# The end of an attention and MoE kernel: one sum in another buffer, the last stores in other queues

## The chip, the cores and the metric

The kernel runs on one core of a Trainium2 chip. The metric is the device time of one execution in microseconds, as a median of several. Before the change it is 204.68 us (three runs, 204.35 to 205.12). The core has a matrix engine (TensorE, PE in the profile; PEld are its weight loads), VectorE (DVE), ScalarE (ACT), GpSimd (POOL) and SyncE (SP), which here only issues DMAs. Each engine works through its own stream of instructions in order, and streams wait for each other by semaphores. DMAs are issued from a stream and then run beside it.

## The reference

There are 8 batches with 8 heads of 512 tokens and 32 state rows, 64 wide. Tokens attend to state rows and state rows to tokens; the results of both go through a two-layer network with a GELU.

```python
scores = scale * np.matmul(x, state.transpose(0, 1, 3, 2))
a = softmax(scores)                    # written out in the reference
xread = np.matmul(a, state)            # 512 rows for each batch and head
sread = np.matmul(softmax(scale * np.matmul(state, x.transpose(0, 1, 3, 2))), x)   # 32 rows
rows = concatenate([xread, sread])     # 8 * 544 = 4352 rows of 512
out = gelu(rows @ w_in) @ w_out        # 512 -> 2048 -> 512
```

The output is 4352 x 512 in float32, 8.9 MB.

## The kernel before

A unit of work is one batch b. For it the kernel builds the attention weights (AT) and a product P of the state with w_in, so that `mm1` gets the hidden rows directly from AT and P; ScalarE's GELU writes them to the tile `g` (128 partitions, 16 blocks of the hidden size, 512 tokens). The second layer multiplies `g` by w_out. From the second unit on this is done by quarters with seven products instead of eight: `X(b, name)` with names "1" to "7" is one product of half the tokens with half the hidden size by half of the output columns (16 matmuls with 256 columns). Some of the products need a sum or difference of two quarters of `g` as their left side. `g_sum(b, names)` makes it on VectorE (1.2 us each) in a tile `gsum` from a pool of three buffers (`apool`); within a unit the order is "5", "6", "7", "3". Sum "3" is made from a quarter of `g` and sum "6". In the last unit sum "3" gets the same buffer as sum "7", which product "7" reads, so the sum waits until product "7" has been read through.

The products gather in PSUM banks. ScalarE copies intermediate states out (`snap`: c2, c4, u, s5), and VectorE adds bank and copy into the output tiles `oh`: `xs[b, "o", 0]` and `xs[b, "o", 1]`, each with two row blocks j and 512 columns. An output quarter is one half tile's left or right 256 columns: 256 KB. `c21` makes the left quarter of half 1 from product "7" and c4, `c22` the right quarter of half 1 from product bank 1 and s5. `x_out` stores quarters over SyncE's queue.

`R(name)` does the same seven products for the 256 rows of state reads, in tiles `osb`, stored by `r_out` over SyncE.

The change is in the last unit, b = 7. Its end is written out by hand (lines 1215 to 1227): sums "5" and "6", product "1", sum "7", R("7"), product "6", sum "3", R("3"), product "7", c21 and its store, then `L5` and `L3`. These two do the products "5" and "3" in three pieces each (`PIECES`): row block 0 with 256 columns, then row block 1 in two halves of 128 columns, so that copies, additions and stores can begin early. In `L5`, ScalarE copies each piece; as soon as a row block is complete, c22 adds it, and 128 KB go out. In `L3`, VectorE adds each piece with u, and the piece goes out: 128, 64 and 64 KB.

The streams of the engines keep the order in which the lines stand, up to small shifts between queues. A DMA on SyncE's or ScalarE's queue is tied to one of eight semaphores in turn, and before it is issued its queue waits until the DMA eight places before has landed. When all work is issued, SyncE waits for every semaphore in a fixed row, and a barrier of all engines ends the program; these records stand at line 1253.

Of the kernel before, what the change touches and what calls it, by code (L numbers as in the profile page):

```python
# [10 lines left out]
BF16 = mybir.dt.bfloat16  # L11
# [6 lines left out]
def kernel(  # L18
# [8 lines left out]
    nc = tc.nc  # L27
# [17 lines left out]
    apool = ctx.enter_context(tc.tile_pool(name="apool", bufs=3))  # L45
# [36 lines left out]
    x4s = [persist.tile([128, SJ, HC, 128], BF16, name=f"x4_{i}") for i in range(2)]  # L82
# [474 lines left out]
    MH = MC // 2  # L557
    NH = d_model // 2
# [23 lines left out]
    left, right = slice(0, NH), slice(NH, d_model)  # L582
# [8 lines left out]
    def g_q(b, h, k):  # L591
        return gs[b][:, MH * k:MH * k + MH, 256 * h:256 * h + 256]

    def chain(name, q, got):
        a11, a12, a21, a22 = q(0, 1), q(0, 0), q(1, 1), q(1, 0)
        return {
            "1": (a11,),
            "2": (a12,),
            "4": (a22,),
            "5": (a21, a22, ALU.add),  # L600
            "6": (got.get("5"), a11, ALU.subtract),
            "7": (a11, a21, ALU.subtract),
            "3": (a12, got.get("6"), ALU.subtract),
        }[name]

    g_lhs = {}

    def g_sum(b, names):
        got = g_lhs.setdefault(b, {})
        for name in names:  # L610
            x, y, op = chain(name, lambda h, k: g_q(b, h, k), got)
            got[name] = apool.tile([128, MH, 256], BF16, name="gsum", tag="gsum")
            nc.vector.tensor_tensor(out=got[name], in0=x, in1=y, op=op)  # L613

    def x_lhs(b, name):
# [16 lines left out]
    def c_tile(name):  # L632
        return cpool.tile([128, 2, NH], FP32, name=name, tag=name)
# [7 lines left out]
    def add(out, x, y):  # L641
        nc.vector.tensor_tensor(out=out, in0=x, in1=y, op=ALU.add)  # L642
# [5 lines left out]
    def X(b, name):  # L648
        bank = BANK[name]
        first = name in "2154"  # L650
        if first:
            xs[b, bank] = otile([128, 2, NH], "xp", bank)
        ps = xs[b, bank]
        x_mm(ps, x_lhs(b, name), w_rhs(name), first)
        if name == "2":
            if b > 1:
                snap(b, "c2", "c2", ps)
        elif name == "4":
            snap(b, "c4", "c4", ps)
        elif name == "1":  # L660
            for h in range(2):
                xs[b, "o", h] = hpool.tile([128, 2, d_model], FP32, name="oh", tag=f"oh{h}")
            add(xs[b, "o", 0][:, :, left], ps, xs[b, "c2"])
            x_out(b, 0, left)
        elif name == "6":
            snap(b, "u", "u", ps)
        elif name == "5":
            snap(b, "s5", "s5", ps)
        elif name == "7":
            if b < B - 2:  # L670
                c22(b)
                c21(b)
                x_out(b, 1)
        elif name == "3":
            add(xs[b, "o", 0][:, :, right], ps, xs[b, "u"])
            x_out(b, 0, right)

    def c22(b, js=slice(0, 2)):
        add(xs[b, "o", 1][:, js, right], xs[b, 1][:, js, :], xs[b, "s5"][:, js, :])
# [4 lines left out]
    def rows_out(h, js, ns, eng):  # L684
        b = B - 1
        rows = out[b * SB:b * SB + S, :].rearrange("(p j) n -> p j n", j=SJ)
        eng.dma_start(
            out=rows[:, 2 * h + js.start:2 * h + js.stop, ns], in_=xs[b, "o", h][:, js, ns]
        )
# [3 lines left out]
    def l_mm(name, first):  # L693
        b = B - 1
        lhs, rhs = x_lhs(b, name), w_rhs(name)
        for j, n0, n1, at in PIECES:
            if first:
                xs[b, "x", j, n0] = otile([128, n1 - n0], "xp", at)
            ps = xs[b, "x", j, n0]
            for m in range(MH):  # L700
                nc.tensor.matmul(  # L701
                    ps,
                    lhsT=lhs[:, m, 128 * j:128 * j + 128],
                    rhs=rhs[:, m, n0:n1],
                    start=(first and m == 0),
                    stop=(m == MH - 1),
                    skip_group_check=True,
                )
            yield ps, j, n0, n1

    def L5():
        b = B - 1
        xs[b, "s5"] = c_tile("s5")
        for ps, j, n0, n1 in l_mm("5", True):
            nc.scalar.copy(out=xs[b, "s5"][:, j, n0:n1], in_=ps)
            if n1 == NH:
                c22(b, slice(j, j + 1))
                rows_out(1, slice(j, j + 1), right, nc.sync)

    def L3():  # L720
        b = B - 1
        for ps, j, n0, n1 in l_mm("3", False):
            add(xs[b, "o", 0][:, j, NH + n0:NH + n1], ps, xs[b, "u"][:, j, n0:n1])
            rows_out(
                0, slice(j, j + 1), slice(NH + n0, NH + n1), nc.scalar if n0 else nc.sync
            )

    sr = {}
# [114 lines left out]
    def R(name):  # L843
        def c_new(n):
            rs[n] = cpool.tile([128, NH], FP32, name="r_" + n, tag="r_" + n)
            return rs[n]

        bank = BANK[name]
        first = name in "2154"
        if first:  # L850
            home = {"2": 1, "4": 2}
            rs[bank] = otile([128, NH], "rp", home[name]) if name in home else ftile([128, NH], "rp")
        ps = rs[bank]
        lhs = chain(name, r_q, {})[0] if name in "124" else rs["lhs"][name]
        rhs = w_rhs(name)
        for m in range(MH):
            nc.tensor.matmul(  # L857
                ps,
                lhsT=lhs[:, m, :],
                rhs=rhs[:, m, :],  # L860
                start=(first and m == 0),
                stop=(m == MH - 1),
                skip_group_check=True,
            )
        snaps = {"2": "c2", "4": "c4", "6": "u", "5": "s5"}
        if name in snaps:
            nc.scalar.copy(out=c_new(snaps[name]), in_=ps)
        elif name == "1":
            for h in range(2):
                rs["o", h] = opool.tile([128, d_model], FP32, name="osb", tag="osb")  # L870
            add(rs["o", 0][:, left], ps, rs["c2"])
        elif name == "7":
            add(rs["o", 1][:, right], ps, rs["s5"])
            add(rs["o", 1][:, left], ps, rs["c4"])
            r_out(1)
        elif name == "3":
            add(rs["o", 0][:, right], ps, rs["u"])
            r_out(0)
# [69 lines left out]
    def read_out_slot(p):  # L948
        c, b, k = B - 2, B - 1, 16 * (B - 1) + 2 * p
        if p == 0:  # L950
            sr_x("34")
            M(k, k + 1)
            g_sum(c, "56")
            SR("3", 0)
            SR("4", 0)
            X(c, "1")
            sr_x("167")
            SR("5", 0)
            SR("2", 0)
            sr_w("7")  # L960
# [6 lines left out]
        if p == 2:  # L967
            M(k, k + 1)
            SR_gelu("6", 0)
            SR("7", 0)  # L970
            SR_gelu("7", 0)
            g_sum(c, "7")
            X(c, "5")
            SR("3", 1)
            SR("4", 1)
            g_sum(c, "3")
# [238 lines left out]
    b = B - 1  # L1215
# [2 lines left out]
    g_sum(b, "7")  # L1218
    R("7")
    X(b, "6")  # L1220
    g_sum(b, "3")
    R("3")
    X(b, "7")
    c21(b)
    x_out(b, 1, left)
    L5()
    L3()


# [28 lines left out]
```

## Time and profile before

| | us |
|---|---|
| median of three runs | 204.68 |
| the profiled execution, whole | 204.74 |
| its span in the profile | 202.84 |
| TensorE busy | 194.0 |
| last matmul ends | 197.99 |
| last addition ends | 198.30 |
| last store issued (SyncE) | 199.13 |
| last landing | 201.48 |

The difference between the whole and the span, 1.9 us, lies outside of what the profile records. All times in the text count from the span's start. A line of a group names the source line, the engine, the operation, the tiles (out<-in), the shape and the count; a trailing [2.82 <-PE xp L623] says that the engine was idle 2.82 us before it and what ended that. SPq and ACTq are the DMA-issuing records of SyncE and ScalarE; the time to landing is from issue until the semaphore has its last count. TensorE's granted clock was 0.998 of full speed.

### The profile page before, as it was taken

To read this page: it belongs to the slowest core of one execution; us is meant where nothing else is said; L and a number is where in the kernel's file an instruction comes from. 1 tells how busy PE (TensorE), PEld (TensorE's weight loads), DVE (VectorE), ACT (ScalarE), POOL (GpSimd) and SP (SyncE) were. 2 spreads that over 40 slices of the span, in tenths; PEclk is the share of its full clock that TensorE was granted. 3 is DMA by queue.
4 is the path that set the end of the run, shared out by engine and by line. 5 is a ranking of instruction groups with operands and counts; after the bars stand their busy time and mean duration, and the time that the engine had idled before them with its cause. 6 is when DMAs were issued, how large, how long until landed. Compare 5 with 4: busy or idle time off the path is not lost.

```text
span 202.8 us, 4863 instructions
## 1 busy us (share of the span) xinstructions
PE 194.0 (96%) x2030; PEld 134.0 (66%) x2035; DVE 140.4 (69%) x235; ACT 142.8 (70%) x260; POOL 49.9 (25%) x63
## 2 busy tenths in 40 slices
PE   7799999999999999999999999999999999999990
PEld 2434544465767677767767677768767888788890
DVE  2953874889987579656996687567846787862760
ACT  3785578698994989678966896779758588555110
POOL 8963503324318434032306100400000000000000
PEclk9999999999999999999999999999999999999999
DMA  6999999987486999460997051701092010210125
GB/s 191 200 169 203 206 199 192 177 161 137 62 144 126 187 110 182 125 160 0 118 143 210 2 121 38 207 3 53 0 132 81 0 52 3 103 55 0 52 74 190
DMA packets 40582, 23.16 MB, mean 114 GB/s; under 512 B 21872, under 2 KB 39152, under 8 KB 40560
## 3 DMA queue, kind: packets, MB, share of 16 engines
q0 software_dynamic: 13984, 8.10, 29.6%
q1 hardware_dynamic: 25888, 14.36, 29.4%
q10 hardware_dynamic: 688, 0.39, 0.6%
q8 instruction: 16, 0.26, 0.5%
q14 instruction: 6, 0.05, 0.1%
HBM read 17.30 MB, written 8.91 MB: 129 GB/s over the span
## 4 chain that ended last, share of the span: by engine, by line
PE 87%; DMA 4%; POOL 4%; ACT 2%; issue 1%; DVE 0%; ACTq 0%; POOLq 0%
PE xp L623 41%; PE hp L506 27%; DMA w_in_bf<-in_moe_w_in_dram 4%; PE op L548 4%; PE sp L791 3%; PE rp L857 3%; PE op L532 2%; PE xp L701 2%; PE p_ps L441 2%; PE pt L333 2%; POOL w_in_bf L105 2%; ACT P L925 1%; PE sr L887 1%; POOL sbd L95 1%; POOL w_out_bf L113 1%
## 5 line engine op out<-in xcount | busy, mean ns | idle before, releaser
L513 ACT ACTIVATE g<-hp 128x512 bf16<-128x512 f32 x124 | 65.8, 608 | 13.7 <-PE hp L506 13.5
L506 PE MATMUL hp<-AT,P 128*128 128x512 bf16 x248 | 61.0, 379 | 0.0
L623 PEld LDWEIGHTS <-gsum 128*128 128x128 bf16 x416 | 40.5, 98 | 9.4 <-issue 0.4
L623 PE MATMUL xp<-ws,gsum 128*128 128x256 bf16 x320 | 38.2, 273 | 0.0
L506 PEld LDWEIGHTS <-P 128*128 128x128 bf16 x248 | 23.4, 98 | 20.8 <-issue 0.6
L623 PEld LDWEIGHTS <-g 128*128 128x128 bf16 x336 | 32.5, 98 | 7.1 <-issue 1.6
L623 PE MATMUL xp<-w_out_bf,g 128*128 128x256 bf16 x224 | 26.7, 272 | 0.3
L235 POOL COPY xo<-xb 128x1024 bf16<-128x1024 bf16 x12 | 13.2, 1127 | 36.3 <-PE sr L887 36.3
L613 DVE TENSOR_TENSOR gsum<-g 128x2048 bf16<-128x2048 bf16 x14 | 17.1, 1220 | 5.1 <-ACT g L513 4.5
L225 POOL COPY x<-xb 128x1024 bf16<-128x1024 bf16 x12 | 12.4, 1066 | 18.5 <-DMA xb<-in_x_dram 18.5
L646 ACT COPY c<-xp 128x512 f32<-128x512 f32 x14 | 8.3, 593 | 8.9 <-ACT g L513 3.9
L623 PE MATMUL xp<-ws,g 128*128 128x256 bf16 x112 | 13.4, 273 | 0.0
L642 DVE TENSOR_TENSOR oh<-xp,c 128x512 f32<-128x512 f32 x14 | 9.6, 685 | 5.4 <-PE xp L623 5.4
L925 ACT CAST P<-p_ps 128x512 bf16<-128x512 f32 x25 | 12.7, 606 | 0.1
L642 DVE TENSOR_TENSOR oh<-xp,u 128x512 f32<-128x512 f32 (+2 forms) x9 | 5.1, 572 | 10.6 <-PE xp L623 10.4
L548 PE MATMUL op<-w_out_bf,g 128*128 128x512 bf16 x44 | 11.1, 380 | 0.5 <-issue 0.3
L623 PE MATMUL xp<-w_out_bf,gsum 128*128 128x256 bf16 x96 | 11.5, 273 | 0.0
L613 DVE TENSOR_TENSOR gsum<-g,gsum 128x2048 bf16<-128x2048 bf16 x7 | 9.1, 1298 | 2.8 <-PE xp L623 2.8
L356 DVE TENSOR_TENSOR a<-e,ics 128x512 bf16<-128x512 bf16 x14 | 10.5, 750 | 0.5
L925 DVE CAST P<-p_ps 128x512 bf16<-128x512 f32 x15 | 9.4, 684 | 1.7 <-PE p_ps L441 1.7
L353 DVE TENSOR_REDUCE cs<-e 128x16 f32<-128x512 bf16 x14 | 9.5, 678 | 0.7 <-ACT e L340 0.7
L441 PE MATMUL p_ps<-w_in_bf,sbd 64*32 64x512 bf16 x248 | 9.2, 380 | 0.2 <-DMA w_in_bf<-in_moe_w_in_dram 0.2
(136 smaller groups left out, 248.6 us busy)
## 6 DMA issues: line engine op xcount, KB each, us to landing
xb<-in_x_dram POOLq DMA_DIRECT2D x7, 512.0 KB, 7.0
out_dram<-oh SPq DMA_DIRECT2D x14, 256.0 KB, 2.7
out_dram<-oh SPq DMA_DIRECT2D x6, 512.0 KB, 2.9
w_in_bf<-in_moe_w_in_dram POOLq DMA_DIRECT2D x6, 256.0 KB, 12.3
out_dram<-osb SPq DMA_DIRECT2D x5, 256.0 KB, 3.0
w_out_bf<-in_moe_w_out_dram POOLq DMA_DIRECT2D x4, 256.0 KB, 9.0
w_out_bf<-in_moe_w_out_dram POOLq DMA_DIRECT2D x2, 512.0 KB, 12.7
x0f<-in_x_dram SPq DMA_DIRECT2D x3, 256.0 KB, 3.8
```

The costliest lines, as they stand in the source:

```text
L225: nc.gpsimd.tensor_copy(out=A.x4[:, :, :, 64 * t:64 * t + 64].rearrange("p j c d -> p c j d"), in_=src[:, t],)
L235: eng.tensor_copy(out=A.xo[:, :, :, 2 + 64 * t:66 + 64 * t].rearrange("p j c d -> p c j d"), in_=src[:, t],)
L353: nc.vector.reduce_sum(out=cs, in_=e4, axis=AX.X)
L356: nc.vector.tensor_tensor(out=A.a[:, :, hs].rearrange("p g (c n) -> p g c n", n=NS), in0=e4, in1=ics[:, :, :].to_broadcast((128, G, 2, NS) ...
L441: nc.tensor.matmul(ps[t][32 * c:32 * c + 32, :], lhsT=sbd[64 * t:64 * t + 64, b, c, 32 * t:32 * t + 32], rhs=w_in_bf[64 * t:64 * t + 64, c ...
L506: nc.tensor.matmul(hp, lhsT=Ps[b][:, t, m * 128:(m + 1) * 128], rhs=atts[b].AT[:, :, t, :], start=(t == 0), stop=(t == 1),)
L513: nc.scalar.activation(out=gs[b][:, m, :], in_=hp, func=AF.Gelu)
L548: nc.tensor.matmul(ops[b, j], lhsT=gs[b][:, m, j * 128:(j + 1) * 128], rhs=w_out_bf[:, m, :], start=(m == 0), stop=(m == MC - 1),)
L613: nc.vector.tensor_tensor(out=got[name], in0=x, in1=y, op=op)
L623: nc.tensor.matmul(ps[:, j - js[0], :], lhsT=lhs[:, m, 128 * j:128 * j + 128], rhs=rhs[:, m, :], start=(first and j == js[0] and m == 0), ...
L642: nc.vector.tensor_tensor(out=out, in0=x, in1=y, op=ALU.add)
L925: copy(out=Ps[b][:, t, f * 512:(f + 1) * 512], in_=ps[t])
```

## The change

Sum "3" of the last unit is written to the tile `x4s[0]`, seen as 8 blocks of 256 columns, and no longer to a buffer of the pool. `x4s[0]` held a rearranged input, and later a sum of w_in quarters for the state rows. The right quarter of half 1 goes out in one transfer of 256 KB after both of its row blocks are added, where two of 128 KB went out before. Of L3's three pieces the first (128 KB) and the last (64 KB) go to ScalarE's queue and the middle one (64 KB) to SyncE's; before, the first two went to SyncE's and the last to ScalarE's.

```diff
-    def g_sum(b, names):
+    def g_sum(b, names, home=None):
         got = g_lhs.setdefault(b, {})
         for name in names:
             x, y, op = chain(name, lambda h, k: g_q(b, h, k), got)
-            got[name] = apool.tile([128, MH, 256], BF16, name="gsum", tag="gsum")
+            if home is None:
+                got[name] = apool.tile([128, MH, 256], BF16, name="gsum", tag="gsum")
+            else:
+                got[name] = home
             nc.vector.tensor_tensor(out=got[name], in0=x, in1=y, op=op)
...
             if n1 == NH:
                 c22(b, slice(j, j + 1))
-                rows_out(1, slice(j, j + 1), right, nc.sync)
+        rows_out(1, slice(0, 2), right, nc.sync)
...
             rows_out(
-                0, slice(j, j + 1), slice(NH + n0, NH + n1), nc.scalar if n0 else nc.sync
+                0,
+                slice(j, j + 1),
+                slice(NH + n0, NH + n1),
+                nc.sync if j == 1 and n0 == 0 else nc.scalar,
             )
...
-    g_sum(b, "3")
+    g_sum(b, "3", x4s[0].rearrange("p j (u c) n -> p (j u) (c n)", u=2))
```

## The prediction

> **What bounds the kernel now.** I read the page's busy shares first, then the chain that ended last and the waits for the last 17 us, then the timeline and the windows of the tail, and last the issues of DMAs with their time to landing.
>
> The page, and then the chain in order of time from 186 us on (start, length, what):
>
> ```profile
> PE 194.0 (96%) x2030; PEld 134.0 (66%) x2035; DVE 140.4 (69%) x235; ACT 142.8 (70%) x260; POOL 49.9 (25%) x63
> ```
> ```profile
> 192.70 1.75 PE xp L623 x16
> 194.44 3.55 PE xp L701 x48
> 197.99 0.02 issue
> 198.01 0.29 DVE oh L642
> ```
>
> TensorE is the bound up to 197.99 us: it has no gap in the tail. The span is 202.84 us (the page rounds to 202.8), so 4.85 us lie behind the last product: one addition, then stores. Only that stretch can give or cost anything unless TensorE itself is made to wait. Next the waits from 186 us on (who waited, for whom, total, times, longest) and the timeline of VectorE, ScalarE's queue and SyncE's queue (start, length, engine, line):
>
> ```profile
> DVE gsum L613 <- PE xp L623: 2.8, 1, 2.8
> ```
> ```profile
> 191.25 0.41 DVE L642 TENSOR_TENSOR osb<-rp,r_c 128x256 f32<-128x256 f32 x1
> ...
> 194.48 1.23 DVE L613 TENSOR_TENSOR gsum<-g,gsum 128x2048 bf16<-128x2048 bf16 x1 [2.82 <-PE xp L623]
> 195.62 0.42 DVE L642 TENSOR_TENSOR osb<-rp,r_u 128x256 f32<-128x256 f32 x1
> 195.96 0.68 DVE L642 TENSOR_TENSOR oh<-xp,c 128x512 f32<-128x512 f32 x1
> 196.55 0.74 DVE L642 TENSOR_TENSOR oh<-xp,s 128x256 f32<-128x256 f32 x2
> 197.22 0.64 DVE L642 TENSOR_TENSOR oh<-xp,u 128x256 f32<-128x256 f32 x2
> 198.01 0.29 DVE L642 TENSOR_TENSOR oh<-xp,u 128x128 f32<-128x128 f32 x1 [0.15 <-PE xp L701]
> ```
> ```profile
> 196.07 0.55 SPq L838 DMA_DIRECT2D out_dram<-osb  x1
> 197.12 0.39 SPq L637 DMA_DIRECT2D out_dram<-oh  x1
> 197.62 1.92 SPq L687 DMA_DIRECT2D out_dram<-oh  x4
> ```
>
> VectorE stood still for 2.82 us (191.66 to 194.48) because the sum "3" is written into the buffer that product "7" is reading. Everything behind it on VectorE was pushed together, and six transfers reached SyncE's queue within 3.1 us (196.07 to 199.13). The windows (stretch, its length, then busy of PE, PEld, DVE, ACT, POOL; clock, DMA share, GB/s):
>
> ```profile
> 196.00:197.00 1.00, 1.00 (x14) 0.91 (x12) 1.00 (x4) 0.33 (x2) 0.00 (x0) 1.00 0.00 0
> 197.00:198.00 1.00, 0.98 (x17) 0.80 (x15) 0.86 (x3) 0.00 (x0) 0.00 (x0) 1.00 0.66 139
> 198.00:199.00 1.00, 0.00 (x0) 0.00 (x0) 0.29 (x1) 0.00 (x0) 0.00 (x0) 1.00 1.00 358
> 199.00:200.00 1.00, 0.00 (x0) 0.00 (x0) 0.00 (x0) 0.00 (x0) 0.00 (x0) 1.00 1.02 341
> 200.00:201.00 1.00, 0.00 (x0) 0.00 (x0) 0.00 (x0) 0.00 (x0) 0.00 (x0) 1.00 0.67 218
> ```
>
> The DMA engines idle in 196 to 197 and are full from 198 to 200: 139 + 358 + 341 + 218 = 1056 KB go out in a backlog after the products are done. What it costs is in the time to landing, first of a 256 KB store alone (189.89), then of the tail (store, engine, size, us to landing):
>
> ```profile
> out_dram<-oh SPq DMA_DIRECT2D x1, 256.0 KB, 2.1
> ```
> ```profile
> out_dram<-oh SPq DMA_DIRECT2D x1, 256.0 KB, 3.0
> ```
> ```profile
> out_dram<-oh ACTq DMA_DIRECT2D x1, 64.0 KB, 2.5
> ```
>
> The same 256 KB need 2.06 us alone and 3.02 us in the tail. Single records of the trace give the rest: the five stores of line 687 were issued at 197.624, 198.164, 198.659, 199.134 (SyncE) and 198.337 (ScalarE), and landed at 200.508, 201.059, 201.298, **201.484** and 200.860. SyncE's closing waits then run one by one, 0.06 us apart: the semaphore of the 199.134 store stands first among those of stores and passes at 201.500, the semaphore of ScalarE's store stands last and passes at 201.929, and the span ends 0.911 us after that.
>
> **The change, part by part.** Times are against the profiled execution: span 202.84 us, 204.74 us in all, 0.06 above the median 204.68.
>
> *The sum in a buffer of its own.* The tile x4s[0] was last read by the SR products, long before; in the built streams the sum keeps its place on VectorE and waits for VectorE alone. So it starts behind the addition that ends at 191.66 and takes 1.23 us: 192.89. Behind it, in order: the addition into osb, 0.42 us, waits for R("3") (TensorE 191.66 + 1.04 = 192.70), so 192.9 to 193.3; its store goes out at 193.35 instead of 196.07. The addition c21 is late next: it needs product "7" (semaphore at 194.457), so 194.48 to 195.16, and its 256 KB store leaves at 195.2 instead of 197.12. The two c22 additions (0.41 us each) now wait for ScalarE's copies (ended 195.73 and 196.52): 195.75 to 196.17 and 196.55 to 196.97 instead of 197.30. L3's first piece is ready at 197.10 by TensorE's semaphore: 197.12 to 197.53 (before: 197.64). The last addition waits for TensorE as before: 198.01 to 198.30. TensorE gains nothing: L3 started at 196.05, after the sum's end at 195.71, without a gap. But 512 KB of the 1056 KB backlog now land by 195.2 + 2.06 = 197.3, before the last products' stores begin.
>
> *One store for the right quarter.* Removes one issue from SyncE's queue (spacing 0.50 to 0.54 us there) and a semaphore; adds a wait of the first row block for the second, 196.17 to 196.97. Behind it on SyncE stands only the 64 KB store, ready at 197.87. Bounds: 0 to 0.04 us gained or lost, since 256 KB issued at 197.0 lands by 197.0 + 2.06 = 199.06 alone, or 200.0 at the 3.02 of the tail; both lie before the last landing. I take 0; the cover is about 1.0 us, and if it were gone the price would be at most the 0.8 us of waiting.
>
> *The last pieces over two queues.* ScalarE issues the 128 KB piece at 197.56 (issue 0.37 to 0.41 us, spacing some 0.5 as on SyncE; the one pair of ScalarE's issues in the trace, 0.739 and 1.256, is 0.52 apart) and is free at 198.08, before the last piece's addition ends: cost 0, cover 0.25 us. SyncE issues the 64 KB piece at 197.88. ScalarE has no computing left behind these issues. So the last issue of all moves from 199.13 (SyncE) to 198.34 (ScalarE), set by TensorE's end.
>
> *Landing of that last 64 KB.* Not shown without a backlog. Upper row: the same store before, 2.52 us, in the full stretch. Lower end: its first packet came 1.01 us after the issue, and the lone 256 KB store's packets ran 0.83 us, so a quarter of that, 0.2, and 0.34 from the end of that store's last packet to its landing give 1.55. Nearest row: the lone 256 KB store with 2.06, which is 0.83 of packets. By the order of bytes ahead (256 KB done near 198.7, then 128 and 64 KB) the engines are almost free at 199.35, so I take 1.75, somewhat above the low end: landing 198.34 + 1.75 = 200.09.
>
> *The closing waits.* The last landing is now that of ScalarE's store, whose semaphore stands last in the closing row, also in the changed program; the other eight waits pass while it is under way (the 64 KB of SyncE lands by 197.88 + 2.06 = 199.94). So 0.911 + 0.02 follow the landing, where 1.356 did (201.484 to 202.84): 0.43 us gained.
>
> **Sum**: span 200.09 + 0.93 = 201.02 against 202.84, so 1.8 us less; with the ends 1.55 and 2.52 for the landing, 2.0 and 1.05 less. From 204.74: 202.9, and 202.7 to 203.7.
>
> **A rule against it.** The row first: SyncE's last issues stand 0.47 to 0.54 us apart, and the DMA engines are full at the same time. The Trainium skill's "DMA: Bandwidth & Descriptors", section "Issuing engines are not separate DMA queues", says that transfers of all issuing engines share the same 16 DMA engines and that spreading issues over queues saves only sequencer time. By it the third part alone, with the backlog left, would keep the last packet near 201, and only the closing waits' 0.43 us would be sure. The trace agrees so far that ScalarE's store took 2.52 us beside SyncE's. The section "Anatomy of one DMA" of the page fits (for another path) 2.0 us plus bytes over 436 GB/s: an estimate of 2.15 us for 64 KB and 2.6 for 256 KB, where the trace's lone store needs 2.06; with 2.15 the gain would be 1.4 us. I go by the trace.
>
> **Rivals.**
>
> *The backlog or the landing stays the limit.* If ScalarE's two stores in a row are served slowly, or the engines are still full at 199.4, the last one takes 2.6 to 3.1 us (the tail's 256 KB row shows 3.02): end 198.34 + 3.02 + 0.93 = 202.29, a gain of 0.55 us, which is within 0.5%. For it: all of the tail's stores took 2.35 to 3.08. Against it: half of the bytes have gone by then.
>
> *The sum does not move* (some other wait holds it until 194.48). Then 1056 KB remain in the backlog and only the queues and the closing waits count. ScalarE's store keeps its 2.52 to 2.9: end 201.8 to 202.2, a gain of 0.7 to 1.05 us. Against it: the stream has no wait for TensorE in front of the sum.
>
> *Slower: the last store on ScalarE lands late.* One of ScalarE's stores that follow each other has one row in this trace: the second load at the start took 4.24 us. With it the end is 198.34 + 4.24 + 0.93 = 203.51, 0.67 us later than before (204.74 to 205.4). It decides from 3.57 us on (202.84 - 0.93 - 198.34). Against it: that row stands among five loads that fill the engines.
>
> **How the numbers follow.** A run of this kernel tells about 0.5%, 1.02 us, from no change. Forecast 0.77 (gain 1.05 to 2.0); landing or backlog 0.14; the sum does not move 0.04; slower 0.05, of which about half over 0.5%. Faster by over 0.5% means a gain of more than about 1.0: the forecast nearly whole and some of the third case give 0.78; slower 0.03; the rest, 0.19, is within 0.5%. The time of the forecast is 204.74 - 1.8 = 202.94, 202.9 against the median. The range starts at the low end of the landing, less the runs' scatter of some 0.2 (202.5), and goes up to the first rival's 204.1.
>
> **What would show it.** The sum on VectorE at 191.7 without a wait for TensorE; c21's store issued near 195.2 with about 2.1 us to landing; DMA busy at 193.5 to 197 and not full at 199 to 200; SyncE's last issue near 197.9 and ScalarE's two near 197.56 and 198.34; the last landing near 200.1; span near 201.0. Wrong it would be if TensorE ended after 198.1 (its weights from the other tile, or a wait), if ScalarE's last store took over 2.5 us, or if the end lay more than 1.0 us behind the landing.

## The result and the profile after

The changed kernel takes 203.06 us (median of six runs, 202.78 to 203.59) where the kernel before takes 204.58: a ratio of 0.9925, 95% interval 0.9907 to 0.9943. Measured once more, beside the experiments, it was 202.51 against 204.53, 0.9900 (0.9878 to 0.9922). The prediction was 202.9 (202.5 to 204.1), faster.

The profiled execution took 203.15 us with a span of 201.32. First the end of the chain in order of time in the kernel after (start, length, what), to be set beside the chain of before:

```profile
193.04 1.75 PE xp L626 x16
194.78 3.55 PE xp L704 x48
198.33 0.02 issue
198.35 0.29 DVE oh L645
```

Product by product it has the same lengths, and TensorE has no gap. All of it stands 0.34 us later than before, and the first store of a tile `osb` already does (38.24 against 37.90 us), long before the first line that the change touches. The timeline of VectorE, SyncE's and ScalarE's queues in the kernel after (start, length, engine, line):

```profile
191.59 0.41 DVE L645 TENSOR_TENSOR osb<-rp,r_c 128x256 f32<-128x256 f32 x1
191.92 1.22 DVE L616 TENSOR_TENSOR x<-g,gsum 128x2048 bf16<-128x2048 bf16 x1
193.07 0.42 DVE L645 TENSOR_TENSOR osb<-rp,r_u 128x256 f32<-128x256 f32 x1
194.88 0.69 DVE L645 TENSOR_TENSOR oh<-xp,c 128x512 f32<-128x512 f32 x1 [1.38 <-PE xp L626]
196.10 0.42 DVE L645 TENSOR_TENSOR oh<-xp,s 128x256 f32<-128x256 f32 x1 [0.53 <-ACT s L718]
196.88 0.42 DVE L645 TENSOR_TENSOR oh<-xp,s 128x256 f32<-128x256 f32 x1 [0.36 <-ACT s L718]
197.46 0.74 DVE L645 TENSOR_TENSOR oh<-xp,u 128x256 f32<-128x256 f32 x2 [0.15 <-PE xp L704]
198.35 0.29 DVE L645 TENSOR_TENSOR oh<-xp,u 128x128 f32<-128x128 f32 x1 [0.15 <-PE xp L704]
```
```profile
192.03 2.05 SPq L844 DMA_DIRECT2D out_dram<-osb  x2
195.60 0.39 SPq L640 DMA_DIRECT2D out_dram<-oh  x1
197.34 1.23 SPq L690 DMA_DIRECT2D out_dram<-oh  x2
```
```profile
197.92 1.12 ACTq L690 DMA_DIRECT2D out_dram<-oh  x2
```

The sum begins right behind the addition in front of it; the wait of 2.82 us for product "7" is gone from the row. What is late next stands in the brackets: c21 waits for TensorE, c22 for ScalarE's copies. The second store of the state rows and that of the left quarter, 512 KB of the former backlog, were issued by 195.6. The windows of the tail in the kernel after (stretch, length, busy of PE, PEld, DVE, ACT, POOL, clock, DMA share, GB/s):

```profile
195.00:196.00 1.00, 1.00 (x17) 0.94 (x15) 0.57 (x1) 0.31 (x1) 0.00 (x0) 1.00 0.74 215
196.00:197.00 1.00, 1.00 (x16) 0.94 (x14) 0.54 (x2) 0.60 (x3) 0.00 (x0) 1.00 0.54 186
197.00:198.00 1.00, 1.00 (x18) 0.97 (x17) 0.83 (x3) 0.00 (x0) 0.00 (x0) 1.00 0.29 92
198.00:199.00 1.00, 0.32 (x6) 0.14 (x3) 0.49 (x2) 0.00 (x0) 0.00 (x0) 1.00 0.79 281
199.00:200.00 1.00, 0.00 (x0) 0.00 (x0) 0.00 (x0) 0.00 (x0) 0.00 (x0) 1.00 0.78 244
200.00:201.00 1.00, 0.00 (x0) 0.00 (x0) 0.00 (x0) 0.00 (x0) 0.00 (x0) 1.00 0.00 0
```

Before, 1056 KB came from 197 us on; now it is 92 + 281 + 244 = 617 KB. The rest goes out earlier, beside the products, and nothing is left after 200. The last store, by its issue in the kernel after (engine, size, us to landing):

```profile
out_dram<-oh ACTq DMA_DIRECT2D x1, 64.0 KB, 1.7
```

Single records give 198.677 for its issue and 200.409 for its landing: 1.732 us where the same store needed 2.523. SyncE's closing waits had all but the last passed by 200.23, and the span ended 0.906 us behind the landing.

To keep the part ahead of the tail out, the measure in what follows is the **tail**: from the end of the last addition on VectorE to the end of the span. It was 198.30 to 202.84 = 4.54 us before, and 198.645 to 201.315 = 2.67 after: 1.87 us less. Each tail is that of one profiled execution; the two of the changed kernel agree to 0.01 us. The medians of whole times are too coarse for the parts: their intervals reach 0.14 to 0.24% (0.3 to 0.5 us) to either side, so what a part is worth is read from the traces. KB left counts the bytes of stores whose packets start after the last product, from the records of DMA packets:

| kernel | tail us | KB left | last landing, us behind the last addition | end, us behind the last landing |
|---|---|---|---|---|
| before | 4.54 | 896 | 3.18 | 1.36 |
| after | 2.67 | 494 | 1.76 | 0.91 |
| the sum alone | 3.03 | 365 | 1.69 | 1.34 |
| the stores alone | 4.21 | 894 | 3.24 | 0.98 |
| two half stores | 3.02 | 385 | 1.67 | 1.36 |
| old queues | 2.66 | 494 | 1.75 | 0.91 |
| one store more | 3.26 | 518 | 1.91 | 1.36 |
| small last piece | 2.80 | 484 | 1.90 | 0.91 |
| half in one store | 3.29 | 712 | 2.30 | 0.99 |
| after, again | 2.66 | 492 | 1.75 | 0.91 |

### The profile page after: what moved, and what is told of

It reads as the page before. It is cut to its first block, busy times and chain, and to the rows that moved or that the text cites. A ratio compares the mean times of both kernels' runs of the same rounds, so it can differ in the third digit from the quotient of the medians.

```text
span 201.3 us, 4865 instructions
## 1 busy us (share of the span) xinstructions
PE 195.5 (97%) x2035; PEld 134.6 (67%) x2035; DVE 140.9 (70%) x235; ACT 142.8 (71%) x260; POOL 49.8 (25%) x63
## 4 chain that ended last, share of the span: by engine, by line
PE 91%; DMA 3%; ACT 2%; DVE 1%; issue 1%; SPq 0%; ACTq 0%
PE xp L626 41%; PE hp L506 27%; PE op L548 5%; PE sp L797 3%; PE rp L863 3%; DMA x0f<-in_x_dram 3%; PE op L532 2%; PE xp L704 2%; PE p_ps L441 2%; PE pt L333 2%; ACT P L931 1%; PE sr L893 1%; PE hp L1041 1%; PE aT_ps L374 1%; ACT sraw L901 1%
## 5 line engine op out<-in xcount | busy, mean ns | idle before, releaser
L548 PE MATMUL op<-w_out_bf,g 128*128 128x512 bf16 x48 | 11.8, 380 | 0.0
L429 DVE COPY XSR<-srT 128x128 bf16<-128x128 bf16 (+1 forms) x5 | 3.4, 671 | 8.7 <-PE srT L424 8.7
```

What stands on the lines that cost most here:

```text
L548: nc.tensor.matmul(ops[b, j], lhsT=gs[b][:, m, j * 128:(j + 1) * 128], rhs=w_out_bf[:, m, :], start=(m == 0), stop=(m == MC - 1),)
```

## The experiments

The theory was that two things make the tail: the backlog on the DMA engines, which the early sum dissolves, and the place of the last store's semaphore in SyncE's closing row of waits. Rivals were that spreading the last stores over two queues brings the gain, that the order of the closing row is of no account, and that VectorE's order counts by itself, without the bytes.

### The sum alone

```diff
 # the changed kernel, with the stores as before
-        rows_out(1, slice(0, 2), right, nc.sync)
+                rows_out(1, slice(j, j + 1), right, nc.sync)
-                nc.sync if j == 1 and n0 == 0 else nc.scalar,
+                nc.scalar if n0 else nc.sync,
```

> Measure: from the end of the last addition on VectorE to the end of the span (before the change 4.54 us, after it 2.67 us). Here only the sum goes to a buffer of its own; the right quarter goes out as two stores and the last pieces stand in the old queues. Theory (the backlog on the DMA engines, and the place of the last store in the closing row of waits): the backlog is gone, so the last 64 KB land 1.7 to 2.0 us after their issue, but with one store more the last one is tied to the semaphore that stands first among those of stores in the closing row, which costs 0.43 us: tail 3.0 to 3.4 us, time about 1.2 us below before. Rival (the gain is from spreading the last stores over two queues): SyncE still issues its stores one behind the other, tail 4.0 us or more, time within 0.5 us of before.

Measured: 203.04 against 204.48 us, 0.9920 (0.9901 to 0.9939); tail 3.03. The issues between 195 and 201 us (engine, count, size, median us to landing):

```profile
out_dram<-oh SPq DMA_DIRECT2D x3, 128.0 KB, 1.9
out_dram<-oh SPq DMA_DIRECT2D x1, 256.0 KB, 2.7
out_dram<-oh SPq DMA_DIRECT2D x1, 64.0 KB, 1.7
out_dram<-oh ACTq DMA_DIRECT2D x1, 64.0 KB, 1.7
```

Four stores still stand one behind the other on SyncE's queue, and both of the last ones land in 1.7 us. So 1.51 of the 1.87 us come from the sum alone, and the old queues are no hindrance. The end came 1.335 us behind the landing: the last store's semaphore stands first among those of stores in the closing row, and seven more waits follow it. The whole time is 1.44 us below before, somewhat more than the 1.2 expected.

### The stores alone

```diff
 # the changed kernel, with the sum back in the pool
-    g_sum(b, "3", x4s[0].rearrange("p j (u c) n -> p (j u) (c n)", u=2))
+    g_sum(b, "3")
```

> Only the stores are changed (one store for the right quarter, the last pieces over both queues); the sum keeps its buffer of the pool and waits for product 7. Theory: the 1056 KB still come as a backlog after 196 us, so the last store needs 2.4 to 2.9 us to land instead of 1.73, but its semaphore stands last in the closing row: tail 3.4 to 3.9 us, time 0.7 to 1.1 us below before. Rival (queues are what counts): tail 2.7 to 2.8 us, as with the whole change.

Measured: 204.32 against 204.48, 0.9987 (0.9970 to 1.0004), not told from no change; tail 4.21. Waits, issues and windows of this kernel:

```profile
DVE gsum L616 <- PE xp L626: 2.8, 1, 2.8
```
```profile
out_dram<-oh SPq DMA_DIRECT2D x2, 256.0 KB, 3.4
out_dram<-osb SPq DMA_DIRECT2D x1, 256.0 KB, 3.0
out_dram<-oh ACTq DMA_DIRECT2D x1, 128.0 KB, 3.0
out_dram<-oh SPq DMA_DIRECT2D x1, 64.0 KB, 3.4
out_dram<-oh ACTq DMA_DIRECT2D x1, 64.0 KB, 2.8
```
```profile
197.00:198.00 1.00, 0.56 (x11) 0.39 (x7) 0.74 (x3) 0.00 (x0) 0.00 (x0) 1.00 0.96 256
198.00:199.00 1.00, 0.00 (x0) 0.00 (x0) 0.00 (x0) 0.00 (x0) 0.00 (x0) 1.00 0.97 342
199.00:200.00 1.00, 0.00 (x0) 0.00 (x0) 0.00 (x0) 0.00 (x0) 0.00 (x0) 1.00 1.10 370
```

The wait is back and with it the full DMA engines. SyncE issued its last store at 197.75, 0.15 us before the last addition's end (197.89), where it was 0.83 us behind it before the change (199.13 and 198.30): 1.0 us earlier. The last landing behind that addition did not come sooner (3.24 against 3.18 us): here the earlier issue only waited longer beside full DMA engines. The rival of the queues falls here. But the tail is 0.3 us over the theory's upper end too: I had taken ScalarE's store for the last, and it was SyncE's 64 KB, behind the merged 256 KB, that landed last (3.38 us). Only the closing row gave something, 0.38 us.

### Two half stores

```diff
-        rows_out(1, slice(0, 2), right, nc.sync)
+                rows_out(1, slice(j, j + 1), right, nc.sync)
```

> The whole change, but the right quarter goes out as two stores of 128 KB as before. Theory: landing of the last store 1.7 to 1.9 us as with the whole change, and 0.43 us more behind it, since one more store moves the last one to the semaphore waited for first: tail 3.0 to 3.2 us. Rival (the row of closing waits does not matter, only the landing): tail 2.65 to 2.8 us. A third possibility, that the merged store itself saves time on SyncE's queue, would show in a later landing of the last store.

Measured: 203.02 against 204.48, 0.9916 (0.9893 to 0.9939); tail 3.02, the last landing even 0.1 us sooner behind the last addition (1.67), the end 1.357 behind it. The merged store saves nothing on its queue; with one store more the closing row costs 0.45 us again.

### Old queues

```diff
-                nc.sync if j == 1 and n0 == 0 else nc.scalar,
+                nc.scalar if n0 else nc.sync,
```

> The whole change, but L3's first piece stays on SyncE's queue as before; the last store keeps its place in the closing row. Theory (the queues add next to nothing once the backlog is gone): SyncE issues the middle piece some 0.2 us later than with the whole change, it lands at about the time of the last one, tail 2.65 to 2.85 us. Rival (spreading over queues is what brought the gain): tail 3.2 us or more.

Measured: 202.94 against 204.48, 0.9914 (0.9889 to 0.9938); tail 2.66. The last pieces' new queues are worth 0.01 us: nothing.

### One store more, elsewhere

```diff
 # in X, name "7", of the changed kernel
-                x_out(b, 1)
+                if b == 3:
+                    x_out(b, 1, left)
+                    x_out(b, 1, right)
+                else:
+                    x_out(b, 1)
```

> The whole change, and one store of the fourth unit (b = 3, some 60 us or more before the end) is cut in two, so that every later store is tied to the next semaphore in turn; the tail's instructions are the same. Theory (the place in the closing row): the last store's semaphore is now waited for first among those of stores, the other seven waits of 0.06 us come after the landing: landing after 1.7 us as with the whole change, 1.34 us behind it instead of 0.91, tail 3.0 to 3.15 us. Rival (the 0.36 us that the kernels with two half stores lost come from the second half store itself): tail 2.6 to 2.75 us.

Measured: 203.30 against 204.53, 0.9949 (0.9926 to 0.9972); tail 3.26, a little over the theory. The tail's instructions are those of the changed kernel; the end came 1.357 us behind the landing and not 0.906. So 0.45 us come from the place in the row alone, and no half store is needed for it. The other 0.15 us are a later landing (1.875 us after the issue); in this execution the left quarter needed 3.46 us and pushed the stores behind it. The records of packets show what ran beside it: a packet of 16 KB of the kind "instruction", 1.45 us long, until 196.84. In all seven profiles in which the left quarter goes out early by itself, it landed 1.46 to 1.51 us after the end of such a packet, and here the packet ran longest. No run was made without the packet, so that it is the cause is read from the records alone.

### A smaller last piece

```diff
-    PIECES = ((0, 0, NH, 2), (1, 0, NH // 2, 0), (1, NH // 2, NH, 3))
+    PIECES = ((0, 0, NH, 2), (1, 0, 3 * NH // 4, 0), (1, 3 * NH // 4, NH, 3))
```

> The whole change, with the second row block of L5 and L3 cut into 192 and 64 columns instead of 128 and 128, so that the last addition and the last store (32 KB) are smaller. If the time behind the last product goes with the size of its last piece: addition 0.2 instead of 0.29 us, landing 1.5 to 1.7 us, 0.1 to 0.25 us less from the last product to the end. If rows of 256 bytes or the narrow matmuls eat that, no difference or up to 0.2 us more.

Measured: 203.08 against 204.53, 0.9920 (0.9905 to 0.9934); tail 2.80, no gain over the change. From the last product's end to the end of the last addition it is 0.29 us (0.33 in the changed kernel, profiled on the same chip), but the last store, issued in the stretch from 197.85 to 198.1:

```profile
out_dram<-oh SPq DMA_DIRECT2D x1, 96.0 KB, 1.8
out_dram<-oh ACTq DMA_DIRECT2D x1, 32.0 KB, 1.9
```

The 32 KB with rows of 256 bytes took 1.864 us, more than the 1.720 of 64 KB with rows of 512. Its packets ran 0.27 us (0.33 for the 64 KB), but the first came 0.98 us after the issue (0.88), and the landing 0.61 us after the last (0.51). Whether the short rows or the traffic beside them lengthened these two, the run does not tell; the smaller piece brought no earlier landing.

### The whole half in one store

```diff
-        rows_out(1, slice(0, 2), right, nc.sync)
+        rows_out(1, slice(0, 2), slice(0, d_model), nc.sync)
...
-    x_out(b, 1, left)
     L5()
```

> The whole change, but the left quarter of half 1 is not stored at 195.6 us by itself: it goes with the right quarter in one store of 512 KB at about 197.3 us. VectorE's work stays where the change put it; only 256 KB are put back into the last stretch. Theory (bytes in the last stretch set the last landing): from the first packets at about 198.2 us 768 KB need 2.1 us at some 370 KB/us, the last store lands 2.1 to 2.5 us after its issue, and one store fewer puts its semaphore one place before the end of the closing row (0.06 us): tail 3.05 to 3.5 us. Rival (VectorE's order alone brings the gain): landing 1.7 to 1.8 us, tail 2.65 to 2.8 us.

One run: 203.73 us; tail 3.29, and 2.27 us from the last issue to its landing, as the theory had them. VectorE has the changed kernel's order, without a wait of the sum, yet the windows and issues show part of the backlog again:

```profile
198.00:199.00 1.00, 0.00 (x0) 0.00 (x0) 0.10 (x1) 0.00 (x0) 0.00 (x0) 1.00 0.97 382
```
```profile
out_dram<-oh SPq DMA_DIRECT2D x1, 512.0 KB, 2.7
out_dram<-oh ACTq DMA_DIRECT2D x1, 128.0 KB, 2.6
out_dram<-oh SPq DMA_DIRECT2D x1, 64.0 KB, 2.5
out_dram<-oh ACTq DMA_DIRECT2D x1, 64.0 KB, 2.3
```

With 712 KB left after the last product where the change has 494, the last landing is 0.54 us later behind the last addition (2.30 against 1.76). Bytes in the last stretch set the end, not VectorE's order by itself.

### The changed kernel again

> The changed kernel once more, on the same chip as the three others, as the measure for them: tail 2.6 to 2.75 us, time 0.6 to 0.9% below before. Its last product's end shows how far the part ahead of the tail scatters between profiled executions (197.6 to 198.4 us so far).

Measured: 202.51 against 204.53, 0.9900 (0.9878 to 0.9922), so 1.0% below before and a little more than expected; tail 2.66, as in the first profile to 0.01 us. The last addition ended at 198.139, where the first profile of the same program had 198.645: 0.51 us of scatter. Of this, 0.42 us stand already at the first store of an osb tile (37.82 against 38.24 us), in the stage of loads.

## Why the prediction was right

*The bound.* Right: TensorE's tail kept its lengths, and the gain lies behind the last product. One sign that the prediction named for being wrong did appear, TensorE ending after 198.1: it ended at 198.33. Neither reason given with it holds, since no product waited or grew longer. The 0.34 us stand already at 38 us, and in the second profile TensorE ended at 197.81.

*The sum.* Right, mechanism and times: it began 0.25 us later than said, with all of the tail 0.34 us later, and c21's, c22's and L3's additions came where the working has them, shifted by that amount, to within 0.1 us. The run with the sum alone shows that this is the main part: 1.51 of 1.87 us. One term was wrong without consequence: the left quarter needed 2.88 us and not 2.06; the records of packets show one of 16 KB of the kind "instruction" that ran 0.96 us beside it, which I had not counted. So it landed at 198.48, after the last product and not before the last stores began, but still 1.9 us before the last store.

*One store for the right quarter at 0.* Half right. On SyncE's queue it is worth nothing, as two half stores show. But the change of its semaphore's place, which the prediction booked under the closing waits as a sum of its own, is its doing: without the merging the last store falls back to the first place, and 0.36 us of tail are lost.

*The last pieces over two queues at 0.* Right: 0.01 us. The page "DMA: Bandwidth & Descriptors" of the Trainium skill, in "Issuing engines are not separate DMA queues", was right for this part, in both states of the DMA engines: with them free, the old queues cost nothing; with them full, issuing SyncE's last store 1.0 us earlier brought no earlier end of the backlog.

*The landing of 64 KB.* 1.75 taken, 1.73 measured (1.64 to 1.73 over the runs with 64 KB last and no backlog, apart from the one store more). The estimate of 2.15 from that page's "Anatomy of one DMA" was too long for this queue; the trace's own rows were the better base. That 1.75 came so close is in part luck: it was a choice somewhat above a low end of 1.01 us to the first packet, 0.2 of packets and 0.34 to the landing, and these measured 0.88, 0.34 and 0.52.

*The closing waits.* 0.93 taken, 0.906 measured; the gain of 0.43 us was 0.45 in the run that moves the place alone.

*The sum of the terms.* The prediction had 198.30 to 201.02, a tail of 2.72 us; measured 2.67 and 2.66. The first median's gain (1.52 us) is smaller than the 1.8 said and the second's (2.02) larger; the intervals of both (1.17 to 1.90 and 1.60 to 2.50 us) hold 1.8. The part ahead of the tail scatters too: the first profile was 0.34 us late there.

*The rivals.* The sum that does not move was given a gain of 0.7 to 1.05 us. It is the run with the stores alone, and it gained 0.32 us of tail. The step that failed there is that ScalarE's store would be the last to land, in 2.5 to 2.9 us. In that run the last to land was the last in the longer queue; this is no rule, for with the half in one store ScalarE's 64 KB landed last (200.40), though SyncE's queue had more bytes (its last landing 200.19). The slow landing of ScalarE's two stores did not come: 2.12 and 1.73 us. The 4.24 us of that rival were those of a 256 KB load at the start, no store.

No kernel tried here is better than the changed one by more than its interval; old queues and the change have the same tail.

## What to carry to other kernels

When a kernel's span goes on for microseconds behind its last product, look at what the DMA engines did while TensorE was still busy: here they idled at 196 us and then had 0.9 MB to send, because one buffer of a small pool held up an in-order engine from 191.66 to 194.48. Give the last stretch its buffers, and send early what is early; here the queue that issued the last stores was worth 0.01 us, and issuing sooner into full DMA engines moved nothing. Count the stores too: if the program closes with a fixed row of waits, the last store should be the one waited for last (0.43 to 0.45 us here).

## What the hardware showed that was not expected

The closing row of nine waits on SyncE costs 0.06 us for each wait that stands behind the last landing, 0.43 to 0.45 us between the first place among the stores and the last; one more store some 95 us before the end shifts it. A store of 32 KB with rows of 256 bytes (1.86 us) landed no sooner than one of 64 KB with rows of 512 (1.72 us). A 256 KB store beside a 16 KB packet of the kind "instruction" took 2.71 to 3.46 us, where alone it took 2.06. And one program's profiled executions differ by 0.5 us at the last addition, of which 0.42 are there after the first 38 us, in the stage of loads.
